# Seven instead of six pairs of hidden blocks by seven products, and the products of the edge rows in the next half's first steps

## The chip, the cores and the metric

The kernel runs on one core of one Trainium2 chip. The metric is the device time of one execution in microseconds (us), as the median of several runs. Five engines work beside each other, each with an instruction queue of its own: TensorE (PE in the profile, with its weight loads as PEld), VectorE (DVE), ScalarE (ACT), GpSimd (POOL) and SyncE (SP), which here issues nearly all transfers between memory and the core.

## What is computed

An attention with packed keys, followed by a gated feed-forward layer. For 8 batches of 8 heads, 576 rows of 64: 32 rows `p` attend to `k`, `v`; then `q` attends to the 32 packed rows. The result, 4608 rows of 512, goes through the feed-forward layer:

```python
p_packed = sm_attn(p, k, v)
out = sm_attn(q, p_packed, p_packed)
...
h = x @ w_in                      # 512 -> 2048
g = h * np.clip(h + 3.0, 0.0, 6.0) / 6.0
return (g @ w_out).astype(np.float32)   # 2048 -> 512
```

All in 32-bit floats. A number of full precision is kept as a high part, rounded to the format that TensorE reads, and a low part, the rest; a product of two such numbers takes three TensorE products (high by high, high by low, low by high).

## The kernel before

**Stages.** The first batch, with the loading and splitting of all weights, follows an order written out by hand (`PLAN`). After it comes a loop over the batches 1 to 7. Each has two *halves*, c = 0 and c = 1, of about 256 rows each, and each half goes through the 16 blocks of 128 hidden columns (d_ff = 2048) in 16 *steps* (`pos` in `moe_pairs`). The attention of the next batch is woven into the steps by `fill`, which calls generators: the loads and transposes of `attention_inputs` in steps 0 to 4 of the first half, then `attention`, and in the second half `u_s2` and the projections of the packed rows (`first_quarters`, with reloads of w_in, `w_again`). Outside the parts marked as manual, the framework orders the instructions of each engine itself when it builds the program, by dependencies and by the order in which they were written; on the chip each engine then follows that order strictly.

**A step.** `first_product` (L922) makes one block of h for the rows of the half: six TensorE products of 256 columns, or 320 in a *wide* half. `gate_into` (L938) applies the gate, on ScalarE and VectorE. Then the block is either a *single* or one of a *pair*:

- A single (`gated`, then `single_product`, L1162): the two blocks of 128 rows are split into high and low parts, and each is multiplied by the block's 512 columns of w_out: six products of 512 columns. They add into the banks A and B.
- A pair of blocks 2i and 2i + 1 (`pair_product`, L1130) is a 2 by 2 block product (two blocks of rows, two blocks of d_ff, two halves of the 512 output columns) by seven products in place of eight: sums of the gated blocks are made on VectorE (L1196, L1204, L1209) and split (`parted`, L949), and 21 products of 256 columns add into the banks A, B, C and D. After the last pair of a half, ScalarE, GpSimd and VectorE read C and D (L1148 to L1160); A and B are read after the last single (L1167).

A product is written out one or two steps after its block was gated (`pend`, `second`). The pairs come first in a half, then the singles: with six pairs, steps 0 to 11 and 12 to 15. The first half takes the pairs in descending order (5 to 0), the second in ascending order. The second half of batch 1 has four pairs, its first half none (`moe`, L1014).

**The combined blocks.** Of the weights of a pair, three sums (T1, T2, T4) have a place of their own, and a fourth (T3) takes the place of a block of w_out. `combine` (L1057) makes them during batch 1. There are four places for T1, T2 and T4, in the buffers that w_in held before, so that four of the pairs take turns in two of them: pairs 0 and 4 in one, 1 and 5 in the other. These four are kept in memory (`t_kept`, L1100), and `fetch_t` (L1103) brings them back, 768 KB each, by two fetches in each half (`FETCHES`, at steps 5 and 7), issued on SP.

**Edge rows.** A batch has 576 rows, 64 more than four blocks of 128. The 64 odd rows of an even batch and those of the odd batch behind it make one block of 128. Their gated columns are collected in `bnd` (`keep_edge`, L964), and in the first half of batches 3, 5 and 7 (`joined`) their products are made: eight *edge steps* of two d_ff blocks each, with parts split by `edge_parts` (L988) into a buffer that the pairs use too (`raw`), and multiplied by `edge_product` (L1000). They are written out between the singles of that half (L1225 to L1240), in the bank of D (in batch 7 in a bank of the attention), which ScalarE reads at the end (L1181).

Of the kernel before, what the change touches and what calls it, by code (L numbers as in the profile page):

```python
# [26 lines left out]
PAIRS = 6  # L27
FIRST_PAIRS = 4
TURN = (
# [3 lines left out]
FETCHES = (((5, 1), (7, 0)), ((5, 4), (7, 5)))  # L33
# [44 lines left out]
def packed_attention_moe(  # L78
# [420 lines left out]
    def u_a(b, x, z):  # L499
# [20 lines left out]
        hi = ap.tile([P, S], F32R, name="a_hi", tag=f"a_hi{x}", bufs=2)  # L520
        lo = ap.tile([P, S], F32R, name="a_lo", tag=f"a_lo{x}", bufs=2)
# [466 lines left out]
    def edge_parts(f, summed):  # L988

        j = xp.tile([P, 6 * P], F32R, name="edge", tag="raw")  # L990
        hi, lo = j[:, :3 * P], j[:, 3 * P:]
# [65 lines left out]
    def combine(i):  # L1057

        if i == 0:
            tiles = [wr.tile([P, 4, 2, H2], F32R, name=f"wt{n}", tag=f"w_in{n}") for n in (1, 2, 3)]  # L1060
            for k, name in enumerate(("T1", "T2", "T4")):
                for pair in range(PAIRS):
                    n, at = ((0, k), (1, k), (2, k), ((2, 0, 1)[k], 3))[pair % 4]
# [35 lines left out]
        if i % 4 < 2:  # L1099
            nc.sync.dma_start(out=t_kept[i % 4 + i // 4 * 2], in_=slots[i % 4].rearrange("p a x m -> p (a x m)"))  # L1100
        yield

    def fetch_t(i):  # L1103
        nc.sync.dma_start(out=slots[i % 4].rearrange("p a x m -> p (a x m)"), in_=t_kept[i % 4 + i // 4 * 2])

    def moe_pairs(b, c, fill):

        pairs = list(range(FIRST_PAIRS if b == 1 else PAIRS))
        if c == 0:
            pairs.reverse()  # L1110
        n_pairs = len(pairs)
        steps = [2 * i + k for i in pairs for k in range(2)] + list(range(2 * n_pairs, NF))
# [10 lines left out]
        edges = []  # L1123
# [6 lines left out]
        def pair_product(i, lhs):  # L1130
# [5 lines left out]
            if i == pairs[0]:  # L1136
                order = order[2:4] + order[:2] + order[4:]
# [34 lines left out]
        def edge_step(f, summed, parts):  # L1172
            if "J" not in made:
                made["J"] = att_pair()[0] if b == B - 1 else acc_of(roles[3])
                first = True
            else:
                first = False
            edge_product(made["J"], f, *parts, summed, first, f == NF - 2)
            if f == NF - 2:
                osb = gp.tile([P, DM], F32, name="osb_j", tag="g", bufs=4)  # L1180
                nc.scalar.activation(out=osb, in_=made["J"], func=AF.Copy, scale=1.0 / 6.0)  # L1181
                nc.sync.dma_start(out=out[b * S - REM:b * S + REM], in_=osb)

        for pos, f in enumerate(steps):
            fill(pos)
            h = first_product(b, f, t0, n)
            if pos < 2 * n_pairs:
                if f % 2 == 0:
# [9 lines left out]
                    second(1)  # L1198
                    continue
# [25 lines left out]
            if joined:  # L1225
                while edges:
                    edges.pop(0)()
            pend.append(lambda f=f, gh=gh, gl=gl: single_product(f, gh, gl))
            second(2)
            if joined:  # L1230
                j = f - 2 * n_pairs
                n_single = NF - 2 * n_pairs
                todo = [(2 * i, True) for i in range(n_pairs) if i * (n_single - 1) // n_pairs == j]
                if j == n_single - 1:
                    todo = [(g, False) for g in range(2 * n_pairs, NF, 2)]
                for g, summed in todo:
                    parts = edge_parts(g, summed)
                    edges.append(lambda g=g, summed=summed, parts=parts: edge_step(g, summed, parts))
        if joined:
            pend[-1:-1] = edges  # L1240
# [132 lines left out]
    t_kept = dram.tile([PAIRS - 2, P, 3 * DM], F32, name="t_kept")  # L1373
# [16 lines left out]
    for b in range(1, B):  # L1390
# [10 lines left out]
        def fill(c, f):  # L1401
            s = c * NF + f
            with behind_gates():
                if b == 1:
# [6 lines left out]
                    for i in range(PAIRS):  # L1411
# [58 lines left out]
```

## Time and profile before

| | before |
|---|---|
| runs | 715.52, 712.47, 714.78 us; median 714.78 us |
| profiled execution | 714.05 us; its span, first to last instruction, 712.2 us |
| mean granted clock of TensorE | 0.99 of full speed |
| instructions | 16078, of them 5906 TensorE products |
| transfers | 107.48 MB, 151 GB/s on average |

How to read the profile's lines: a group's line names the program's line, engine, operation, what is written and read, the shapes and the count; behind the bar stand its busy time in us, the mean of one in ns, and the idle time of the engine just before it with what ended it. A timeline's line has the start and the length in us, and behind the instruction in brackets the idle time before it. The chain is the sequence of work that ended last, followed back from the last instruction. A stretch's line has busy us and counts of PE, PEld, DVE, ACT and POOL, then the granted clock and the transfers. TensorE's products overlap, and their ends are modelled, so that their starts tell more than their lengths. `acc<-wt,gf` is a product of a pair that reads a combined block, `acc<-wo_hi,g` one of a single, `acc<-wo_hi,edge` one of an edge step.

### The profile page before, as it was taken

What the parts mean: (1) busy time and instruction counts of PE and PEld (TensorE: products, weight loads), DVE (VectorE), ACT (ScalarE), POOL (GpSimd) and SP (SyncE); (2) the same over time, 40 slices, a digit from 0 to 9 for tenths busy, and PEclk for the clock granted to TensorE, in tenths of its full rate; (3) what the DMA queues carried; (4) which work ended last, traced back from release to release, by engine and by line L of the source; (5) the groups of instructions that cost most, each with busy time, mean ns of one, the idle gap of its engine ahead of it and who ended that gap; (6) DMA issues with size and microseconds to landing.
All of it is one profiled execution on the core that took longest, in us unless ns stands there. A gap on an engine that the chain in (4) does not pass through costs nothing.

```text
span 712.2 us, 16078 instructions
## 1 busy us (share of the span) xinstructions
PE 691.6 (97%) x5906; PEld 594.8 (84%) x5906; DVE 532.0 (75%) x1169; ACT 428.6 (60%) x1013; POOL 353.6 (50%) x539
## 2 busy tenths in 40 slices
PE   6699999999999999999999999999999999999997
PEld 5477876888878888899798988899888898889997
DVE  3888788587899779786598867888488876975453
ACT  4798876556565655665366655657356564756453
POOL 1456642555353454465353534556354444547553
PEclk9799999999999999999999999999999999999999
DMA  9969953855327756474554657375543745331030
GB/s 264 338 153 273 217 149 119 258 152 117 108 106 196 169 137 209 118 175 76 129 193 136 161 116 222 109 154 139 130 164 119 165 122 178 119 134 46 30 105 29
DMA packets 199102, 107.48 MB, mean 151 GB/s; under 512 B 173424, under 2 KB 185200, under 8 KB 195440
## 3 DMA queue, kind: packets, MB, share of 16 engines
q1 hardware_dynamic: 198480, 106.26, 54.4%
q8 instruction: 46, 0.75, 0.5%
q14 instruction: 32, 0.26, 0.1%
q10 hardware_dynamic: 544, 0.20, 0.1%
HBM read 89.65 MB, written 16.78 MB: 149 GB/s over the span
## 4 chain that ended last, share of the span: by engine, by line
PE 87%; DVE 6%; DMA 4%; ACT 1%; issue 1%; SPq 1%; POOL 0%; DVEq 0%; ACTq 0%
PE acc L969 48%; PE ps_hh L929 23%; PE ps L350 5%; PE ps_h L607 4%; PE ps L969 2%; PE ps L470 1%; DMA nat<-in_k_dram 1%; DMA wt<-t_kept 1%; PE ps L440 1%; DVE tr L555 1%; PE ps_t L678 1%; DMA k_nat<-in_k_dram 1%; SPq L294 1%; PE ps L273 1%; DMA w_again<-w_kept 1%
## 5 line engine op out<-in xcount | busy, mean ns | idle before, releaser
L929 PE MATMUL ps_hh<-a_hi,m_hi 128*128 128x320 f32 (+1 forms) x448 | 134.8, 301 | 1.5 <-PE acc L969 0.8
L929 PE MATMUL ps_hh<-a_lo,m_hi 128*128 128x320 f32 (+1 forms) x448 | 133.9, 299 | 0.0
L929 PE MATMUL ps_hh<-a_hi,m_lo 128*128 128x320 f32 (+1 forms) x448 | 133.4, 298 | 0.0
L941 DVE SCALAR_TENSOR_TENSOR t<-t,ps_hh 128x320 f32<-128x320 f32 (+1 forms) x148 | 66.0, 446 | 58.9 <-ACT t L940 58.3
L947 POOL TENSOR_TENSOR gf<-tb,gf 128x256 fp32r<-128x256 f32 x76 | 64.6, 851 | 87.4 <-ACT gf L946 56.2
L969 PE MATMUL acc<-wo_hi,g 128*128 128x512 f32 x288 | 103.1, 401 | 0.0
L940 ACT ACTIVATE t<-ps_hh,three 128x320 f32<-128x320 f32 (+1 forms) x148 | 73.9, 500 | 35.0 <-PE ps_hh L929 29.0
L929 PEld LDWEIGHTS ps_hh<-a_hi,m_hi 128*128 128x128 f32 x448 | 85.2, 190 | 10.0 <-issue 3.0
L929 PEld LDWEIGHTS ps_hh<-a_lo,m_hi 128*128 128x128 f32 x448 | 85.2, 190 | 6.5 <-issue 3.5
L929 PEld LDWEIGHTS ps_hh<-a_hi,m_lo 128*128 128x128 f32 x448 | 85.1, 190 | 2.9 <-issue 2.5
L947 POOL TENSOR_TENSOR g<-t,g 128x256 fp32r<-128x256 f32 x72 | 55.7, 775 | 45.4 <-ACT g L946 23.3
L969 PE MATMUL acc<-wt,ga 128*128 128x256 f32 x456 | 74.6, 284 | 0.2
L969 PE MATMUL acc<-wo_hi,ge 128*128 128x256 f32 x304 | 71.5, 286 | 0.2
L947 POOL TENSOR_TENSOR ga<-t,ga 128x256 fp32r<-128x256 f32 x76 | 62.4, 821 | 13.6 <-ACT ga L946 12.3
L969 PEld LDWEIGHTS acc<-wt,ga 128*128 128x128 f32 x456 | 63.0, 190 | 3.3 <-ACT ga L946 1.7
L969 PEld LDWEIGHTS acc<-wo_hi,g 128*128 128x128 f32 x288 | 53.0, 189 | 13.7 <-POOL g L947 3.0
L969 PEld LDWEIGHTS acc<-wo_hi,ge 128*128 128x128 f32 x304 | 52.9, 189 | 8.6 <-ACT t L940 2.1
L965 POOL COPY bnd<-t 128x64 f32<-128x64 f32 x76 | 23.0, 302 | 70.2 <-DVE t L941 64.4
L969 PE MATMUL acc<-wo_lo,g 128*128 128x512 f32 x144 | 56.9, 395 | 0.0
L555 DVE STREAM_TRANSPOSE tr<-nat 128x576 f32<-128x576 f32 x56 | 42.3, 764 | 17.4 <-DMA nat<-in_q_dram 11.8
L940 ACT ACTIVATE tb<-ps_hh,three 128x256 f32<-128x256 f32 (+1 forms) x76 | 37.8, 498 | 19.5 <-PE ps_hh L929 18.5
L946 ACT CAST g<-t 128x256 fp32r<-128x256 f32 x72 | 29.2, 407 | 33.6 <-DVE t L941 33.0
(222 smaller groups left out, 1840.4 us busy)
## 6 DMA issues: line engine op xcount, KB each, us to landing
w_again<-w_kept SPq DMA_DIRECT2D x24, 1024.0 KB, 4.9
wt<-t_kept SPq DMA_DIRECT2D x24, 768.0 KB, 5.4
out_dram<-osb SPq DMA_DIRECT2D x33, 256.0 KB, 2.5
nat<-in_k_dram SPq DMA_DIRECT2D x112, 72.0 KB, 3.2
nat<-in_q_dram SPq DMA_DIRECT2D x112, 72.0 KB, 2.7
raw_in<-in_moe_w_in_dram SPq DMA_DIRECT2D x10, 512.0 KB, 5.2
raw_out<-in_moe_w_out_dram SPq DMA_DIRECT2D x10, 512.0 KB, 5.3
w_kept<-w_in_sb SPq DMA_DIRECT2D x4, 1024.0 KB, 9.4
```

Source lines behind the costliest of these rows:

```text
L273: nc.tensor.matmul(banks[x][NPK * a:NPK * a + NPK, :n * P], state["pp"][half, NPAIR * x + a], cols[half, :, a], start=True, stop=True,)
L294: nc.sync.dma_start(out=t[r:r + 32], in_=src[b, 2 * a + h, :, 32 * c:32 * c + 32].rearrange("(t i) j -> i t j", i=32),)
L350: nc.tensor.matmul(pair[x][NPK * a:NPK * a + NPK, :n], rows[half, a], c, start=True, stop=True)
L555: nc.vector.transpose(out=t, in_=state.pop(("nat", which, b, a)))
L607: nc.tensor.matmul(h[:, hf, :HS], mm[:, g, fs], aa[:, hf * HS:(hf + 1) * HS], start=(g == 0 and i == 0), stop=(g == NG - 1 and i == 2),)
L929: state["first"] = nc.tensor.matmul(h[:, :n], mm[:, g, fs], aa[:, t0:t0 + n], start=(g == 0 and i == 0), stop=(g == NG - 1 and i == 2),)
L940: state["relu"] = nc.scalar.activation(out=t[:, :n], in_=h, func=AF.Relu, bias=three)
L941: state["gate"] = nc.vector.scalar_tensor_tensor(out=t[:, :n], in0=t[:, :n], scalar=6.0, in1=h, op0=ALU.min, op1=ALU.mult)
L946: nc.scalar.copy(out=hi, in_=x)
L947: engine.tensor_sub(out=lo, in0=x, in1=hi.bitcast(F32))
L965: nc.gpsimd.tensor_copy(out=bnd[:, f, side * REM:side * REM + REM], in_=t[:, boff:boff + REM])
L969: nc.tensor.matmul(out, lhs[x], rhs[y], start=first and i == 0, stop=last and i == 2, skip_group_check=True)
```

## The change

- `PAIRS` goes from 6 to 7: the halves of batches 2 to 7 have seven pairs and two singles, but for the first half of batch 2, which keeps six and four, since pair 6 is combined in its steps 12 to 15 (`TURN_LAST`). The order is 5 to 0, then 6 in the first half; 6, then 0 to 5 in the second.
- `PLACE` says which of the four places a pair's blocks have: pairs 0 and 4 share one, 2, 5 and 6 another, and 1 and 3 keep theirs. Five pairs are kept in memory (`KEPT`). There are three fetches in a half: at step 5 pair 2 in both halves, at step 7 pair 0 or 4, at step 11 pair 6 or 5.
- The products of the edge rows are no longer written out in the first half of batches 3, 5 and 7. `owe`, at the end of that half, makes a list of the eight edge steps, and `owed` issues one, two and three of them in the first three steps of the next half and the rest in the fourth. Their parts lie in the buffers of the next batch's attention weights (`a_hi`, `a_lo`), which are empty until then.
- The first pair of a half makes its product for D fourth instead of second.

```diff
-PAIRS = 6
+PAIRS = 7
 FIRST_PAIRS = 4
+PLACE = (1, 3, 0, 2, 1, 0, 0)
+KEPT = (0, 2, 4, 5, 6)
...
+TURN_LAST = (12, 12, 12, 13, 13, 14, 15)
...
-FETCHES = (((5, 1), (7, 0)), ((5, 4), (7, 5)))
+FETCHES = (((5, 2), (7, 0), (11, 6)), ((5, 2), (7, 4), (11, 5)))
+EDGES = (1, 2, 3)
...
-        hi = ap.tile([P, S], F32R, name="a_hi", tag=f"a_hi{x}", bufs=2)
-        lo = ap.tile([P, S], F32R, name="a_lo", tag=f"a_lo{x}", bufs=2)
+        hi, lo = state.pop(("a_room", b, x), None) or (
+            ap.tile([P, S], F32R, name=f"a_{z}", tag=f"a_{z}{x}", bufs=2) for z in ("hi", "lo")
+        )
...
-        if i % 4 < 2:
-            nc.sync.dma_start(out=t_kept[i % 4 + i // 4 * 2], in_=slots[i % 4].rearrange("p a x m -> p (a x m)"))
+        if i in KEPT:
+            nc.sync.dma_start(out=t_kept[KEPT.index(i)], in_=slots[PLACE[i]].rearrange("p a x m -> p (a x m)"))
...
+    def owe(b, pairs):
+
+        rooms = []
+        for x in range(2):
+            t = [ap.tile([P, S], F32R, name=f"a_{z}", tag=f"a_{z}{x}", bufs=2) for z in ("hi", "lo")]
+            rooms.append([z[:, :3 * P] for z in t])
+            if b < B - 1:
+                state["a_room", b + 1, x] = t
+        todo = [(2 * i, True) for i in pairs] + [(f, False) for f in range(0, NF, 2) if f // 2 not in pairs]
...
+        for i, (f, summed) in enumerate(todo):
+            def prepared(i=i, f=f, summed=summed):
+                parts = edge_parts(f, summed, rooms[i % 2])
+                return lambda: edge(f, summed, parts, i)
+            edges.append(prepared)
+        for _ in range(2):
+            ready.append(edges.pop(0)())
+
+    def owed(count):
+
+        while ready and count:
+            count -= 1
+            ready.pop(0)()
+            if edges:
+                ready.append(edges.pop(0)())
...
-        pairs = list(range(FIRST_PAIRS if b == 1 else PAIRS))
-        if c == 0:
-            pairs.reverse()
+        last = PAIRS - 1
+        if b == 1:
+            pairs = list(range(FIRST_PAIRS))
+        elif c == 0:
+            pairs = list(range(last - 1, -1, -1)) + [last] * (b > 2)
+        else:
+            pairs = [last] + list(range(last))
...
-                order = order[2:4] + order[:2] + order[4:]
+                order = order[2:3] + order[:2] + order[3:]
...
                 pend.append(lambda i=f // 2, lhs=lhs: pair_product(i, lhs))
+                if pos >= len(EDGES):
+                    owed(NF)
                 second(1)
+                if pos < len(EDGES):
+                    owed(EDGES[pos])
                 continue
...
+            if joined and pos == NF - 1:
+                owe(b, pairs)
...
                     for at, i in FETCHES[c]:
-                        if f == at:
+                        if f == at and (b, c, i) != (2, 0, PAIRS - 1):
                             fetch_t(i)
+                    if b == 2:
+                        for _ in range(TURN_LAST.count(s)):
+                            next(turned[PAIRS - 1], None)
```

More of the change, by code (lines that the diff above doesn't have):

```diff
@@ L986, in acc_of, with edge_parts @@
         return ps_o.tile([P, DM], F32, name="acc", tag=f"acc{i}", bufs=1)
-    def edge_parts(f, summed):
-        j = xp.tile([P, 6 * P], F32R, name="edge", tag="raw")
-        hi, lo = j[:, :3 * P], j[:, 3 * P:]
+    def edge_parts(f, summed, rooms=None):
+        if rooms:
+            hi, lo = rooms
+        else:
+            j = xp.tile([P, 6 * P], F32R, name="edge", tag="raw")
+            hi, lo = j[:, :3 * P], j[:, 3 * P:]
         raw = bnd[:, f:f + 2]
@@ L1062, in combine @@
                 for pair in range(PAIRS):
-                    n, at = ((0, k), (1, k), (2, k), ((2, 0, 1)[k], 3))[pair % 4]
+                    n, at = ((0, k), (1, k), (2, k), ((2, 0, 1)[k], 3))[PLACE[pair]]
                     blocks[pair, name] = [tiles[n][:, at, x] for x in range(2)]
@@ new lines, in packed_attention_moe, with edge @@
+    edges, ready = [], []
+    def owe(b, pairs):
[6 more added lines that the diff above has]
+        todo = [(2 * i, True) for i in pairs] + [(f, False) for f in range(0, NF, 2) if f // 2 not in pairs]
+        made = []
+        def edge(f, summed, parts, i):
+            if not made:
+                made.append(att_pair()[0] if b == B - 1 else acc_of(roles[3]))
+            acc, = made
+            done = i == len(todo) - 1
+            edge_product(acc, f, *parts, summed, i == 0, done)
+            if done:
+                osb = gp.tile([P, DM], F32, name="osb_j", tag="g", bufs=4)
+                nc.scalar.activation(out=osb, in_=acc, func=AF.Copy, scale=1.0 / 6.0)
+                nc.sync.dma_start(out=out[b * S - REM:b * S + REM], in_=osb)
+        for i, (f, summed) in enumerate(todo):
[5 more added lines that the diff above has]
+            ready.append(edges.pop(0)())
@@ L1111, in moe_pairs @@
+    def owed(count):
[4 more added lines that the diff above has]
+                ready.append(edges.pop(0)())
+    def moe_pairs(b, c, fill):
+        last = PAIRS - 1
[3 more added lines that the diff above has]
+            pairs = list(range(last - 1, -1, -1)) + [last] * (b > 2)
+        else:
+            pairs = [last] + list(range(last))
         n_pairs = len(pairs)
-        steps = [2 * i + k for i in pairs for k in range(2)] + list(range(2 * n_pairs, NF))
+        steps = [2 * i + k for i in pairs for k in range(2)]
+        steps += [f for f in range(NF) if f not in steps]
@@ L1170, in single_product @@
                     nc.sync.dma_start(out=out[row + k * P:row + (k + 1) * P], in_=r)
[L1172 to L1182, printed above, removed]
         for pos, f in enumerate(steps):
@@ L1198, in moe_pairs @@
                     second(1)
+                    owed(EDGES[pos] if pos < len(EDGES) else 0)
                     continue
@@ L1372, in packed_attention_moe @@
     w_kept = dram.tile([NCH, P, FPC * DM], F32, name="w_kept")
-    t_kept = dram.tile([PAIRS - 2, P, 3 * DM], F32, name="t_kept")
+    t_kept = dram.tile([len(KEPT), P, 3 * DM], F32, name="t_kept")
     def keep_w_in(n):
@@ L1410, in fill @@
                                 keep_w_in(n)
-                    for i in range(PAIRS):
+                    for i in range(PAIRS - 1):
                         for _ in range(TURN[i].count(s)):
```

19 lines of the change are left out of this document (2 added, 17 removed).

## The prediction, made before the change was run

> **What bounds the kernel now.** I read the page first: the busy shares and the chain that ended last.
>
> ```profile
> span 712.2 us, 16078 instructions
> PE 691.6 (97%) x5906; PEld 594.8 (84%) x5906; DVE 532.0 (75%) x1169; ACT 428.6 (60%) x1013; POOL 353.6 (50%) x539
> ...
> PE 87%; DVE 6%; DMA 4%; ACT 1%; issue 1%; SPq 1%; POOL 0%; DVEq 0%; ACTq 0%
> ```
>
> TensorE is busy 97% of the span and holds 87% of the chain. Its instructions overlap in this trace, so the busy share alone proves little. What shows the bound is the chain in order of time (start, length, what): in the steady part one group of products begins where the one before ends. I take from it the price of the two things that the change exchanges, and two more rows for later.
>
> ```profile
> 232.77 6.04 DMA wt<-t_kept
> ...
> 243.56 2.52 PE acc L969 x21
> ...
> 247.23 1.39 PE acc L969 x6
> ...
> 274.91 2.49 PE acc L969 x21
> ...
> 380.62 1.38 PE acc L969 x6
> ...
> 404.00 1.44 PE ps_hh L929 x12
> ```
>
> Six products of 512 columns (one block's second product in a half) take 1.38 or 1.39 us. The 21 products of 256 columns that replace two such blocks take 2.49 or 2.52 us. Starts follow columns: 1.385 / 6 = 0.231 us for 512, 2.505 / 21 = 0.119 us for 256. So the kernel is a queue of TensorE products, and a change pays by the products that it takes out of the queue, less the waits that it puts in.
>
> **The change part by part.**
>
> *The seventh pair.* Batches 2 to 7 have twelve halves. All but the first half of batch 2 (still six) get a seventh pair: 11 times two blocks' singles go, 2 x 1.385 = 2.77 us, and one pair comes, 2.505 us. That saves 0.265 us each, 2.9 us in all. By the extreme rows it is 11 x (2.76 - 2.52) = 2.6 to 11 x (2.78 - 2.49) = 3.2 us. The first products of both blocks stay as they are.
>
> The page "TensorE: Matmul & The Clock Gate" of the Trainium skill, section "Back-to-back issue gap", speaks against this: it gives a sustained spacing of 81 ns at 128 columns and 131 ns at 512. An estimate from that page, on a line between its two figures, is 98 ns at 256 columns: 21 x 98 = 2.05 us against 12 x 131 = 1.57 us, a loss of 0.48 us per pair and 5.3 us in all. The trace disagrees with it: 231 ns at 512 columns, 119 at 256.
>
> *VectorE, ScalarE, GpSimd for the seventh pair.* The groups by line and shape (busy us, mean ns) of narrow halves:
>
> ```profile
> L1209 DVE TENSOR_TENSOR tb<-tb,t 128x128 f32<-128x128 f32 x76 | 44.6, 587 | 1.4
> ...
> L947 DVE TENSOR_TENSOR ge<-t,ge 128x256 fp32r<-128x256 f32 x76 | 36.8, 484 | 10.8 <-ACT ge L946 9.2
> ...
> L1204 DVE TENSOR_TENSOR t<-t,tb 128x256 f32<-128x256 f32 x76 | 35.4, 466 | 0.8
> ...
> L941 DVE SCALAR_TENSOR_TENSOR t<-t,ps_hh 128x256 f32<-128x256 f32 x72 | 29.6, 412 | 21.9 <-ACT t L940 21.6
> ...
> L1196 DVE TENSOR_TENSOR t<-t 128x128 f32<-128x128 f32 x76 | 24.1, 317 | 2.0
> ...
> L1076 DVE TENSOR_TENSOR wt<-wx,wt 128x256 fp32r<-128x256 f32 x18 | 7.9, 439 | 3.2 <-ACT wt L1075 2.9
> ```
>
> Two singles cost VectorE two gates, 0.82 us. A pair costs two gates and four more instructions: 0.82 + 0.587 + 0.484 + 0.466 + 0.317 = 2.68 us. So 1.86 us are added per half, where the busiest half is a second one (c = 1) with the next batch's attention. The stretches of 5 us there (PE, PEld, DVE, ACT, POOL busy):
>
> ```profile
> 447.00:452.00 5.00, 5.00 (x48) 4.16 (x48) 5.00 (x12) 2.71 (x9) 3.68 (x6) 1.00 0.54 192
> 452.00:457.00 5.00, 5.00 (x36) 4.76 (x35) 4.18 (x8) 4.18 (x10) 2.97 (x6) 1.00 0.06 23
> 457.00:462.00 5.00, 5.00 (x37) 3.33 (x36) 3.01 (x8) 2.82 (x6) 2.21 (x6) 1.00 0.31 92
> ```
>
> VectorE is full to 452 us, while TensorE still loses nothing. The seventh pair falls into the next two rows, which leave 0.82 + 1.99 = 2.81 us idle. That covers 1.86 us, so I cost it at nothing; if the cover is gone, it is 1.86 us in each of six second halves, 11.2 us. ScalarE gets four casts for two, GpSimd three subtractions for two; at 60% and 50% of the span I cost both at nothing.
>
> *Pair 6 is combined once,* in steps 12 to 15 of batch 2's first half: 11 more VectorE instructions of about 0.44 us (the L1076 row), 4.8 us, beside the four singles that stay in that half. Nothing, at most 4.8 us if none of it were hidden.
>
> *Edge rows.* Three times (batches 3, 5, 7) one of eight edge steps turns from six products of 512 columns into three of 512 and six of 256: 3 x 0.231 + 6 x 0.119 - 1.385 = 0.02 us each, 0.1 us together. Where the steps run hardly changes. The TensorE timeline of batch 3, and ScalarE's read of the sum:
>
> ```profile
> 331.58 0.28 PE L929 MATMUL ps_hh<-a_hi,m_hi 128*128 128x256 f32 x1
> ...
> 332.30 0.40 PE L969 MATMUL acc<-wo_hi,edge 128*128 128x512 f32 x1
> ```
> ```profile
> 353.71 0.60 ACT L1181 ACTIVATE osb_j<-acc 128x512 f32<-128x512 f32 x1 [1.59 <-PE acc L969]
> ```
>
> The 256-column first product of 331.58 us belongs to the next half. So the edge products run in the next half's first steps today: the order that the framework builds had already put them there. The new place of their parts frees a buffer of the pairs, for which TensorE did not wait in these rows. The sum's bank must be read before the first pair's fourth product uses it; the new order puts nine products of 0.119 us in front, 1.07 us for a read of 0.60 us. Nothing; at most 0.6 us three times.
>
> *The fetches.* They grow from 24 to 35, and one more store. What hurts is when each is needed. In a first half the fetch at step 5 now brings pair 2, used as the fourth pair, where before it brought pair 1, the fifth. It stands on SP behind the attention loads of five steps. SP's timeline, batches 4 and 6, then TensorE's first product that reads a fetched place, in the fourth pair of its half in batches 2, 4 and 6 (234.97, 402.16, 569.34), and in the fifth of batch 2 (238.86); then the page's transfers:
>
> ```profile
> 397.19 1.27 SPq L409 DMA_DIRECT2D v_nat<-in_v_dram  x2
> 398.56 1.83 SPq L1104 DMA_DIRECT2D wt<-t_kept  x2
> ...
> 566.39 1.02 SPq L1104 DMA_DIRECT2D wt<-t_kept  x2
> ```
> ```profile
> 234.97 0.52 PE L969 MATMUL acc<-wt,gf 128*128 128x256 f32 x3
> ...
> 238.86 0.62 PE L969 MATMUL acc<-wt,gf 128*128 128x256 f32 x3 [0.26 <-DMA wt<-t_kept]
> ...
> 402.16 0.52 PE L969 MATMUL acc<-wt,gf 128*128 128x256 f32 x3
> ...
> 569.34 0.52 PE L969 MATMUL acc<-wt,gf 128*128 128x256 f32 x3
> ```
> ```profile
> w_again<-w_kept SPq DMA_DIRECT2D x24, 1024.0 KB, 4.9
> wt<-t_kept SPq DMA_DIRECT2D x24, 768.0 KB, 5.4
> ```
>
> Issued as now, the fetch of batch 2 lands at 232.77 + 6.04 = 238.81, 3.84 us after the fourth pair wants it at 234.97. In batch 4 it lands at 398.56 + 5.4 = 403.96 for 402.16, 1.80 us late; in batch 6 at 571.79 for 569.34, 2.45 us late. Batches 3 and 5 I take at the mean of the last two, 2.1 each (an estimate); batch 7 has no attention to load. Together 12.3 us late, if nothing else changes. Against it: 12 of a pair's 21 products read no fetched place (12 x 0.119 = 1.43 us), and the next two steps' 12 first products, 1.44 us by the row at 404.00, can stand in front. The framework orders the queue when it builds it, and did so freely (edge products, above). If it knows of the late landing, 2.87 us of cover hides all but 3.84 - 2.87 = 0.97 us in batch 2. If it doesn't, the queue waits, as in the row of 238.86. From 0 to 12.3 us I take 1.0 us, since the rows around it show a queue without gaps, and keep both ends.
>
> The new fetch at step 11 (pair 5 in second halves, 6 in first) must land before step 15. In first halves SP is idle by then. In second halves it may stand behind a w_again load. The time that it has is two pairs, by TensorE's timeline of batch 4:
>
> ```profile
> 446.62 0.40 PE L969 MATMUL acc<-wt,gf 128*128 128x256 f32 x2
> ...
> 451.63 0.40 PE L969 MATMUL acc<-wt,gf 128*128 128x256 f32 x2
> ```
>
> One pair is 5.01 us, two are 10.0; the two transfers, end to end, are 4.9 + 5.4 = 10.3 us. Nothing, at most 0.3 us in six halves, 1.8 us.
>
> *The end.* Two singles instead of four now follow the last pair. Its last product, the last of the three reads of banks C and D, and the last reads of A and B:
>
> ```profile
> 701.29 0.28 PE L969 MATMUL acc<-wo_hi,ga 128*128 128x256 f32 x1
> ```
> ```profile
> 703.69 0.42 DVE L1153 SCALAR_TENSOR_TENSOR osb<-acc,osb 128x256 f32<-128x256 f32 x1
> ```
> ```profile
> 707.89 1.38 DVE osb L1167 x2
> ```
>
> The reads of C and D ended at 704.11, 2.7 us after the last pair's last product had gone in (701.29 + 0.12), long before those of A and B could start at 707.89. With two singles behind the pair, A's last product has gone in 2.77 - 0.69 = 2.08 us after it, so the reads of C and D end up to 0.6 us late. Part of their 2.7 us is a gate that VectorE will have done earlier. I take 0.2 us, from 0 to 0.6.
>
> **The sum:** -2.9 + 0.1 + 0.2 + 1.0 = -1.6 us. The profiled execution took 714.05 us (span 712.2 and 1.85 around it), so 712.45 on its own terms. It lay 0.73 us below the median shown, 714.78; for the median I say 713.2.
>
> **Rivals.**
>
> *The fourth pair waits for its fetch* (slower). For: the three late sums above, and a queue that stands still at 238.86 with products behind it that need no fetch. Against: the order may be rebuilt around it. The gain before this wait is 2.6 us; beyond that it is slower than before. Half of the 12.3 us uncovered gives 714.78 - 2.6 + 6.2 = 718.4, all of it 724.5.
>
> *VectorE becomes the bound of second halves.* For: 5.00 of 5 us to 452. Against: the two rows after it. Half a microsecond in six halves eats the gain: 715.2; all 11.2 us would be 723.4.
>
> *All is hidden.* 2.9 or 3.2 us less: 711.6 to 711.9.
>
> *Weight loads, one per product, set the spacing:* then 21 loads for 12 lose. For: loads are busy 84% of the span. Against: six products take 1.385 us, not the 0.71 of six at 0.119. Were it so, nine more loads of 0.119 us in 11 pairs cost 11.8 us: 726.6. The page of the Trainium skill cited above is the case for it.
>
> *The change doesn't do what it says* only in its second part: the edge products stay about where they are.
>
> **How the numbers follow.** About 0.5% (3.6 us) is what a measurement of this kernel can tell from no change: below 711.2 is faster, above 718.4 slower. The forecast with small waits, 711.9 to 715, has 0.58; all hidden 0.14; VectorE 0.10; the fetch wait 0.16; loads 0.02. Faster: even the full gain reaches 711.6 only, so it needs the spread of runs (712.47 to 715.52 before) on its side: 0.20. Slower: the fetch wait, mostly, and the loads: 0.17. Same: 0.63. The range starts a microsecond under the full gain, 710.6, and goes past the half-uncovered fetch, 719.0; outside it lies the fully uncovered one.
>
> **What would show it.** Right: 2 x 11 x 6 = 132 fewer 512-column products on `g`, 231 more of 256; 35 fetches; the first fourth-pair fetch product with at most a microsecond of wait. Wrong: a releaser "DMA wt" of many microseconds on TensorE or its loads in first halves (the fetch), gaps ending on VectorE or ScalarE around steps 10 to 15 of second halves, a 21-product row far from 2.5 us, or a tail over half a microsecond longer.

## The result, and the profile after

| | before | after |
|---|---|---|
| median of 6 runs | 713.54 us (712.11 to 715.52) | 721.32 us (720.37 to 725.59) |
| profiled execution, its span | 714.05, 712.2 us | 721.55, 719.8 us |
| ratio | | 1.0121, 95% interval 1.0088 to 1.0153 |

The change makes the kernel 7.8 us slower, outside the range given (710.6 to 719.0). (One execution of e9 below and the traced one of e14 ran far longer than the others of their kernels; the ratios leave them out, and no trace of e14 is read.) Two lines of the page's head, the chain's shares, and the group of products that read the fetched places:

```profile
span 719.8 us, 16493 instructions
...
PE 691.9 (96%) x6014; PEld 599.8 (83%) x6014; DVE 552.8 (77%) x1227; ACT 436.8 (61%) x1042; POOL 364.5 (51%) x555
...
PE 72%; DVE 12%; DMA 8%; ACT 3%; issue 2%; SPq 2%; POOL 1%; DVEq 0%; ACTq 0%; POOLq 0%
...
L977 PE MATMUL acc<-wt,gf 128*128 128x256 f32 x261 | 54.5, 286 | 6.7 <-DMA wt<-t_kept 6.7
```

TensorE's share of the chain falls from 87% to 72%, VectorE's and the transfers' rise to 12% and 8%. The products themselves are what was forecast. First the products of singles and one group of those of pairs before, then after (a line's products by tile: count, ns, first and last start):

```profile
L969 PE MATMUL acc<-wt,ga x456: 274/283/387, 178.7 to 700.9; 128*128 128x256 f32 x152
...
L969 PE MATMUL acc<-wo_hi,g x288: 387/394/502, 123.9 to 708.2; 128*128 128x512 f32 x144
...
L969 PE MATMUL acc<-wo_lo,g x144: 387/394/496, 124.1 to 707.9; 128*128 128x512 f32 x144
```
```profile
L977 PE MATMUL acc<-wt,ga x522: 276/283/415, 178.8 to 711.8; 128*128 128x256 f32 x174
...
L977 PE MATMUL acc<-wo_hi,g x200: 387/394/502, 124.0 to 714.8; 128*128 128x512 f32 x100
...
L977 PE MATMUL acc<-wo_lo,g x100: 388/394/496, 124.2 to 714.6; 128*128 128x512 f32 x100
```

(288 + 144) - (200 + 100) = 132 products of 512 columns are gone; `acc<-wt,ga` has 66 more, six for each of 11 pairs, so 231 of 256 columns have come. Against them stand these five starts on TensorE's timeline, one in the first half of each of batches 2 to 6, and the sum of the weight loads' waits for the same thing (us, times, longest):

```profile
238.14 0.39 PE L977 MATMUL acc<-wt,gf 128*128 128x256 f32 x1 [1.35 <-DMA wt<-t_kept]
...
317.03 0.39 PE L977 MATMUL acc<-wt,gf 128*128 128x256 f32 x1 [0.61 <-DMA wt<-t_kept]
...
406.33 0.39 PE L977 MATMUL acc<-wt,gf 128*128 128x256 f32 x1 [1.35 <-DMA wt<-t_kept]
...
486.38 0.39 PE L977 MATMUL acc<-wt,gf 128*128 128x256 f32 x1 [1.51 <-DMA wt<-t_kept]
...
576.51 0.39 PE L977 MATMUL acc<-wt,gf 128*128 128x256 f32 x1 [1.89 <-DMA wt<-t_kept]
```
```profile
PEld acc L977 <- DMA wt<-t_kept: 7.8, 5, 2.1
```

In starts of products the five waits are 7.5 us (1.51 + 0.77 + 1.51 + 1.67 + 2.05: the distance to the product before, less the usual one of its kind); before there was one of 0.4 us. All five stand at the fourth pair, for pair 2. Why the fetch is late is seen on SP's timeline of batch 4 (start, length, how many issues):

```profile
387.09 1.96 SPq L301 DMA_DIRECT2D nat<-in_k_dram  x4
389.14 0.92 SPq L1225 DMA_DIRECT2D out_dram<-osb  x2
390.15 1.00 SPq L426 DMA_DIRECT2D v_nat<-in_v_dram  x2
391.24 2.32 SPq L301 DMA_DIRECT2D nat<-in_k_dram  x4
393.66 2.07 SPq L301 DMA_DIRECT2D nat<-in_q_dram  x4
395.77 1.79 SPq L426 DMA_DIRECT2D v_nat<-in_v_dram  x2
397.67 2.06 SPq L301 DMA_DIRECT2D nat<-in_q_dram  x4
399.78 1.27 SPq L416 DMA_DIRECT2D v_nat<-in_v_dram  x2
401.14 6.88 SPq L1115 DMA_DIRECT2D wt<-t_kept  x3
```

SP does not pause: 24 issues in the 14.05 us from 387.09 to 401.14, 0.59 us each, and the fetch is the 25th. It lands 5.1 us later, at 406.28, and the waiting product starts at 406.33.

What covers a late fetch can be counted on TensorE. In every one of the five halves the fourth pair has issued its three products on `wo` and `gf` when it wants the fetched place. In batch 4 the third of them, and the last product ahead of the waiting one, are

```profile
403.62 0.29 PE L977 MATMUL acc<-wo_hi,gf 128*128 128x256 f32 x1
...
404.69 0.28 PE L937 MATMUL ps_hh<-a_hi,m_lo 128*128 128x256 f32 x1
```

so the place is wanted at 403.62 + 0.12 = 403.74, and the fetch is 2.54 us late. In batches 2 to 6 the five fetches are 3.50, 1.24, 2.54, 1.86 and 3.09 us late, 12.2 us together. Between the third product and the waiting one stand 17, 4, 9, 2 and 9 others: 41 x 0.119 = 4.9 us of cover. The difference, 7.3 us, is what TensorE waits (7.5 in starts).

The end is longer too. The reads of A, then C or D, then B:

```profile
714.55 0.69 DVE L1222 SCALAR_TENSOR_TENSOR osb<-acc,osb 128x512 f32<-128x512 f32 x1 [0.23 <-PE acc L977]
...
714.81 0.40 PE L977 MATMUL acc<-wo_hi,g 128*128 128x512 f32 x1
715.16 0.41 DVE L1208 SCALAR_TENSOR_TENSOR osb<-acc,osb 128x256 f32<-128x256 f32 x1
...
715.68 0.69 DVE L1222 SCALAR_TENSOR_TENSOR osb<-acc,osb 128x512 f32<-128x512 f32 x1
```

The third read of C and D (L1208) now falls between those of A and B (L1222). From TensorE's last start to the end of the span it is 719.76 - 714.81 = 4.95 us; before it was 712.23 - 708.15 = 4.08. Half of the difference is this order: the last read ends 1.56 us after TensorE's last start (714.81 to 716.37), before it was 1.12. The other 0.4 us lie behind the last read; no run explains them.

So the account is -2.9 (products) + 7.1 (more waits for fetches) + 0.9 (end) = +5.1 us of the 7.8. Some 3 us more were still to be found.

### The profile page after: what moved, and what is told of

Same layout as the page of the kernel before. It is cut to its first block, busy times and chain, and to the rows that moved or that the text cites. A ratio compares the mean times of both kernels' runs of the same rounds, so it can differ in the third digit from the quotient of the medians.

```text
span 719.8 us, 16493 instructions
## 1 busy us (share of the span) xinstructions
PE 691.9 (96%) x6014; PEld 599.8 (83%) x6014; DVE 552.8 (77%) x1227; ACT 436.8 (61%) x1042; POOL 364.5 (51%) x555
## 4 chain that ended last, share of the span: by engine, by line
PE 72%; DVE 12%; DMA 8%; ACT 3%; issue 2%; SPq 2%; POOL 1%; DVEq 0%; ACTq 0%; POOLq 0%
PE acc L977 39%; PE ps_hh L937 19%; PE ps L357 4%; DMA wt<-t_kept 4%; PE ps_h L615 3%; DMA nat<-in_k_dram 2%; PE ps L977 2%; SPq L301 1%; PE ps L477 1%; DVE t L949 1%; DMA w_again<-w_kept 1%; DVE wt L1087 1%; DVE tr L563 1%; DMA raw_in<-in_moe_w_in_dram 1%; PE ps_t L686 1%
## 5 line engine op out<-in xcount | busy, mean ns | idle before, releaser
L955 POOL TENSOR_TENSOR gf<-tb,gf 128x256 fp32r<-128x256 f32 x87 | 74.2, 853 | 124.2 <-ACT gf L954 85.9
L977 PE MATMUL acc<-wt,ga 128*128 128x256 f32 x522 | 87.2, 287 | 0.2 <-ACT ga L954 0.2
L977 PE MATMUL acc<-wo_hi,ge 128*128 128x256 f32 x348 | 82.6, 285 | 0.9 <-ACT ge L954 0.8
L977 PEld LDWEIGHTS acc<-wt,ga 128*128 128x128 f32 x522 | 72.7, 191 | 7.2 <-POOL bnd L973 2.5
L977 PE MATMUL acc<-wo_hi,g 128*128 128x512 f32 x200 | 71.2, 398 | 0.0
L977 PEld LDWEIGHTS acc<-wo_hi,ge 128*128 128x128 f32 x348 | 61.0, 190 | 9.3 <-ACT gf L954 4.2
L977 PE MATMUL acc<-wt,gf 128*128 128x256 f32 x261 | 54.5, 286 | 6.7 <-DMA wt<-t_kept 6.7
L954 ACT CAST ge<-t 128x256 fp32r<-128x256 f32 x87 | 35.3, 405 | 25.0 <-DVE t L1239 23.4
L955 DVE TENSOR_TENSOR ge<-t,ge 128x256 fp32r<-128x256 f32 x87 | 42.3, 486 | 10.5 <-ACT ge L954 9.8
L954 ACT CAST gf<-tb 128x256 fp32r<-128x256 f32 x87 | 35.3, 405 | 24.0 <-DVE tb L949 22.4
```

What stands on the lines that cost most here:

```text
L954: nc.scalar.copy(out=hi, in_=x)
L955: engine.tensor_sub(out=lo, in0=x, in1=hi.bitcast(F32))
L977: nc.tensor.matmul(out, lhs[x], rhs[y], start=first and i == 0, stop=last and i == 2, skip_group_check=True)
```

## The experiments

All differ from the changed kernel, or from the one before where that is said, by the lines shown. Times are medians; the ratio is to the kernel before on the same chip.

| | us | ratio (95% interval) |
|---|---|---|
| e1_fetch_step4 | 713.60 | 1.0011 (0.9992 to 1.0029) |
| e2_pair2_fifth | 717.44 | 1.0066 (1.0042 to 1.0090) |
| e3_edges_only | 712.86 | 0.9993 (0.9976 to 1.0009) |
| e4_six_fourth | 719.33 | 1.0085 (1.0054 to 1.0115) |
| e5_early_cd | 713.35 | 1.0013 (0.9997 to 1.0030) |
| e6_three_places | 714.14 | 1.0025 (1.0010 to 1.0039) |
| e7_three_cd | 713.09 | 1.0011 (0.9996 to 1.0026) |
| e8_fetch_act | 723.65 | 1.0187 (1.0154 to 1.0220) |
| e9_seven_no_fetch | 712.98 | 1.0007 (0.9988 to 1.0026) |
| e10_six_no_fetch | 712.89 | 0.9991 (0.9973 to 1.0010) |
| e11_early_cd_pool | 712.23 | 0.9992 (0.9976 to 1.0007) |
| e12_t_last | 723.10 | 1.0146 (1.0106 to 1.0187) |
| e13_six_more_vector | 720.86 | 1.0107 (1.0091 to 1.0123) |
| e14_seven_no_fetch_pool | 709.30 | 0.9934 (0.9917 to 0.9952) |
| e15_three_cd_pool | 713.69 | 1.0008 (0.9993 to 1.0023) |
| e16_early_cd_pool_all | 710.53 | 0.9955 (0.9941 to 0.9969) |
| e17_six_pool | 713.49 | 1.0000 (0.9986 to 1.0015) |
| e18_cd_pool_late | 719.76 | 1.0107 (1.0073 to 1.0140) |

### Is it the late fetch?

**Issue it a step earlier.**

```diff
-FETCHES = (((5, 2), (7, 0), (11, 6)), ((5, 2), (7, 4), (11, 5)))
+FETCHES = (((4, 2), (7, 0), (11, 6)), ((5, 2), (7, 4), (11, 5)))
```

> The changed kernel with the fetch of pair 2 in first halves at step 4 instead of 5, so that it is issued ahead of two of the attention loads; nothing else. Fetch theory: the five waits on the fetch in batches 2 to 6 (7.5 us together) fall to under 2 us and the time falls by 5 to 7 us, to about 715. Rival (the seventh pair's vector work, the moved edge steps and the end make the loss, and TensorE would only wait for something else at the same place): the waits on the fetch go, others of like size take their place, and the time stays above 719.

713.6 us: 7.7 less than the changed kernel, and no wait on a fetch is left in its trace. But it is not faster than before (713.31 beside it): the 2.9 us do not show.

**Let pair 2 come fifth.**

```diff
-            pairs = list(range(last - 1, -1, -1)) + [last] * (b > 2)
+            pairs = [5, 4, 3, 1, 2, 0] + [last] * (b > 2)
...
-FETCHES = (((5, 2), (7, 0), (11, 6)), ((5, 2), (7, 4), (11, 5)))
+FETCHES = (((5, 2), (7, 0), (12, 6)), ((5, 2), (7, 4), (11, 5)))
```

> The changed kernel with first halves taking their pairs in the order 5, 4, 3, 1, 2, 0, 6, so that the pair that is fetched at step 5 comes fifth, as before the change, and the pair that has a place of its own comes fourth; the fetch of pair 6 moves from step 11 to 12, behind the use of its place. Fetch theory: the same as with the earlier issue, 5 to 7 us less, about 715, with under 1 us of waits on the fetch, though the fetch is issued as late as in the changed kernel. Rival: above 719. If pair 6's later fetch comes too late, a new wait on a fetch stands at the last pair of first halves.

717.44: half a hit. The waits on fetches fall to 0.3 us, but TensorE waits for something new (its waits: us, times, longest):

```profile
PE ps L477 <- DMA v_high<-in_v_dram: 1.9, 5, 0.6
```

In starts of products of this form 3.6 us are lost. The fetch moved to step 12 is now issued ahead of the loads of q and v of the next stage.

**One thing of the change in the kernel before.**

```diff
+PLACE = (1, 3, 0, 2, 1, 0)
+KEPT = (0, 2, 4, 5)
-FETCHES = (((5, 1), (7, 0)), ((5, 4), (7, 5)))
+FETCHES = (((5, 2), (7, 0)), ((5, 4), (9, 5)))
...
```

> The kernel before with one thing of the change: its four places are dealt out so that in first halves the pair fetched at step 5 is pair 2, the fourth, and not pair 1, the fifth. Six pairs, edge steps as before, two fetches in each half (in second halves the one of pair 5 at step 9, since its place is free later). Fetch theory: waits on the fetch of 6 to 8 us in batches 2 to 6 and a time of 719 to 722, slower than before without a seventh pair. Rival: about 714, and the waits only appear along with the seventh pair.

719.33, six pairs all the same. Its waits:

```profile
PE acc L971 <- DMA wt<-t_kept: 6.4, 5, 3.3
```

So the late fetch alone costs 6 us and needs no seventh pair.

**The edge steps alone:** six pairs with places, fetches and order of before (`PAIRS = 6`, `PLACE = (0, 1, 2, 3, 0, 1)`), and `owe`, `owed` and the product for D fourth as in the change.

> Only the second part of the change: six pairs with the fetches, places and order of before, the edge steps issued in the next half's first steps and the first pair's product for D fourth. If the moved edge steps cost nothing, as predicted: 712.5 to 714.5. If they are part of the loss (one stall in each of three halves and the parts made later), 715 or more.

712.86, as before. The moved edge steps are out of it.

### Queue or transfers, and what covers the fetch

**The fetch on another queue.**

```diff
...
-                            fetch_t(i)
+                            fetch_t(i, nc.scalar if (c, at) == (0, 5) else nc.sync)
```

> The changed kernel with the fetch at step 5 of first halves issued on ScalarE's queue instead of SP's; where it is written stays the same. If it is SP's queue that makes the fetch late (some twenty issues of about half a microsecond stand ahead of it): the fetch starts some microseconds earlier, the waits of 7.5 us fall to under 3, and the time to 715 to 717. If it is the transfers themselves (the memory side full with the loads): it starts earlier and lands no earlier, and the time stays at 719 to 722.

723.65, worse than the change. The fetch of batch 2 on ScalarE's queue, then VectorE:

```profile
225.78 0.36 ACTq L1115 DMA_DIRECT2D wt<-t_kept  x1
...
232.48 0.78 DVE L563 STREAM_TRANSPOSE tr<-nat 128x576 f32<-128x576 f32 x1 [3.74 <-DMA nat<-in_k_dram]
```

It is issued 6.6 us earlier than in the changed kernel (232.37 there), and TensorE waits for no fetch. But its 768 KB now move beside the small loads of k: the last of these, issued at 225.71, lands at 232.35, 6.6 us later (in the changed kernel 226.00 and 229.77, 3.8 us). The transpose that stands at the head of VectorE's queue idles 3.74 us for it, the gates behind it are late, and TensorE waits 2.8 us for one there. In all, its waits for gates are 10.1 us in starts, for 1.5 in the changed kernel: 8.6 us more, where the fetch had cost 7.5. Neither of the two expectations names this. The Trainium skill, page "DMA: Bandwidth & Descriptors", section "Issuing engines are not separate DMA queues", says that transfers of all issuing engines run on the same 16 DMA engines and interleave, and that another issuer saves only the time of issuing. This trace agrees: the issue is 6.6 us earlier, and the loads pay. The section also calls the issue time usually small beside the transfer. So it is here for one transfer, 0.59 us for 5.1; it is 24 issues in a row that take 14 us.

The early fetch of e1 has a like chain on a smaller scale, VectorE first, then TensorE:

```profile
395.10 0.78 DVE L563 STREAM_TRANSPOSE tr<-nat 128x576 f32<-128x576 f32 x1 [1.28 <-DMA nat<-in_k_dram]
395.80 0.38 DVE L949 SCALAR_TENSOR_TENSOR tb<-tb,ps_hh 128x256 f32<-128x256 f32 x1
```
```profile
396.24 0.39 PE L937 MATMUL ps_hh<-a_hi,m_hi 128*128 128x256 f32 x1 [0.45 <-DVE tb L949]
```

But most of this is not the fetch: in e9 below, without any fetch, the same transpose waits 1.06 us (at 393.67) and TensorE 0.23 behind it.

**Products that need no fetch first.**

```diff
+            if i != pairs[0]:
+                order = [order[k] for k in (0, 2, 3, 6, 1, 4, 5)]
```

> The changed kernel with the products of all pairs but the first of a half in another order: the four that read no fetched place first, the three that read T4, T1 and T2 last. The fetches stay at step 5. In the changed kernel only the three products of A12 and B21 stand ahead of T4; now twelve do, nine more of 0.119 us, 1.07 us of cover in each pair. If TensorE follows the written order inside a pair, each of the five waits of 0.77 to 2.05 us falls by 1.07 us, to 2.6 us in all, and the time by 4.9 us, to 716 to 717. If the order in which the queue is built already covers what it can, no change: 720 to 722.

723.1: no gain, but the new order did not arrive on TensorE where it was meant to. Batch 4 on TensorE and on SP:

```profile
407.00 0.52 PE L977 MATMUL acc<-wt,gf 128*128 128x256 f32 x2 [1.72 <-DMA wt<-t_kept]
```
```profile
401.89 1.02 SPq L1115 DMA_DIRECT2D wt<-t_kept  x2
```

Ahead of the waiting product stand the same products as in the changed kernel: three of the pair on `gf`, three on `ga` and six first products of a later step. It is so in batches 2 and 6 too; in batch 3 one fewer stands there, in batch 5 one more. The order that the framework builds had kept its place for the fetched products, so whether more cover would help was not tested. In batch 4 the fetch came 0.75 us later and the wait is as long as before; the five waits are 5.9 us in starts instead of 7.5, and the time does not follow.

### Where do the saved products go?

**Three places taking turns,** so that the four pairs in place come first in every half (e6); then with C and D first in a half's last pair (e7, the second piece of code). e5 has this order with the early fetch of e1.

```diff
-PLACE = (1, 3, 0, 2, 1, 0, 0)
-KEPT = (0, 2, 4, 5, 6)
+PLACE = (1, 3, 0, 2, 1, 0, 2)
+KEPT = (0, 2, 3, 4, 5, 6)
...
-FETCHES = (((5, 2), (7, 0), (11, 6)), ((5, 2), (7, 4), (11, 5)))
+FETCHES = (((5, 2), (7, 0), (9, 6)), ((5, 3), (7, 4), (9, 5)))
...
-            pairs = list(range(last - 1, -1, -1)) + [last] * (b > 2)
+            pairs = [5, 4, 3, 1, 2, 0] + [last] * (b > 2)
...
-            pairs = [last] + list(range(last))
+            pairs = [6, 0, 2, 1, 3, 4, 5]
```
```diff
+            if i == pairs[-1]:
+                order = order[2:6] + order[:2] + order[6:]
```

> The changed kernel with three instead of two of the four places taking turns, first halves in the order 5, 4, 3, 1, 2, 0, 6 and second halves 6, 0, 2, 1, 3, 4, 5, with fetches at steps 5, 7 and 9: in every half the four pairs that are in place come first, each fetch is needed two or more pairs after it is issued, and in first halves the fetch at step 5 stays behind the attention loads on SP. Theory (SP's queue has room for the fetch only behind those loads; ahead of them it delays the gates through VectorE, at step 12 it delays the loads of v): waits on fetches under 0.5 us, waits on a transpose at the head of VectorE as before the change, no wait on v; so the 2.9 us of the seven products show: 711.5 to 712.5 with the longer end, 1 to 2 under before. Rival (VectorE is full with the seventh pair and TensorE waits for gates wherever the fetch is): 713 to 715 with 2 us or more of waits on gates.

> The one with three places taking turns, and in the last pair of every half the products for C and D ahead of those for A and B. Theory: 0.7 to 1.0 us under the one with three places, 710.5 to 711.7, faster than both kernels. Rival: no better than three places alone.

> The changed kernel with the fetch of pair 2 at step 4, and in the last pair of every half the four products for C and D ahead of the three for A and B. Theory (the longer end comes from the reads of C and D, which start 9 products too late now that two singles follow the last pair): A's last read is no longer followed by a wait for the third read of C and D, the time from the last product's start to the end falls from 5.0 to about 4.2 us, and the time is 0.7 to 1.0 us under the one with the early fetch alone, about 712.8. Rival (the end is set by the last product and the store): the end stays at 5.0 us, no change.

All three miss their times: 714.14, 713.09 and 713.35, none faster than before. The part on the end can be seen in the traces only: from TensorE's last start to the end 4.4 us in e5 (4.96 without the order), 4.3 in e7 (4.7 in e6); the runs do not separate half a microsecond. In e15, e16 and e18 below, which have this order too, it is 4.6 to 4.7.

**No fetch at all,** with seven pairs and with six (`pass` in place of `fetch_t(i)`).

> The changed kernel without any of its 35 fetches, so that four of the seven pairs are multiplied by weights of other pairs; all else as in the changed kernel. The longest wait that fetches can cause, on TensorE or through delayed loads on VectorE, is gone. Theory (what is left of the loss with the early fetch comes from the transfers): about 2 us under the kernel before without its fetches (2.9 us of products saved, 0.9 us of a longer end). Rival (it comes from VectorE's extra work in the seventh pair): within 1 us of it, with waits of TensorE on gates of 2 us or more.

> The kernel before without any of its 24 fetches, so that two of the six pairs are multiplied by weights of other pairs; the counterpart of the changed kernel without fetches. Both theories: the kernel before waited 0.4 us for fetches, so 0 to 1.5 us less than before, 711.5 to 713; its distance to the other is what tells.

712.98 and 712.89: without a single fetch, seven pairs are still no faster than six. So the transfers are not what keeps the gain. TensorE's waits for gates, with seven, then with six:

```profile
PE ps_hh L937 <- DVE tb L949: 1.5, 5, 0.4
```
```profile
PE ps_hh L929 <- DVE tb L941: 0.4, 1, 0.4
```

In starts, all waits that end on a gate of VectorE are 1.1 us in the kernel before, 1.1 with six pairs here and 2.6 with seven. Five of the six with seven pairs stand in first halves, 13 to 16 us after the batch's first product.

**More work on VectorE alone,** in the kernel before: five instructions on unused columns, at steps 12 and 13.

```diff
+            if b > 1 and f in (12, 13):
+                a1, a2, a = (t[:, off + i * P:off + j * P] for i, j in ((0, 1), (1, 2), (0, 2)))
+                if f == 12:
+                    nc.vector.tensor_sub(out=t[:, W:W + P], in0=a2, in1=a1)
+                nc.vector.tensor_add(out=t[:, W:W + 2 * P], in0=a, in1=a)
+                nc.vector.tensor_sub(out=t[:, W:W + 2 * P], in0=a, in1=a)
```

> The kernel before with five more VectorE instructions in the first two singles (steps 12 and 13) of each half from batch 2 on, about 2.2 us in each half by the rows of such instructions (0.317 and 4 x 0.466), on columns that nothing reads. VectorE theory: the gates behind them come late in the batches with attention; 1.5 to 4 us more than before, 714 to 717. Rival (VectorE has room for it, as predicted): within 0.7 us of before.

720.86: 7.5 us slower, nearly twice the highest expected. The groups of the added instructions, and a stretch of VectorE and TensorE in batch 5:

```profile
L1232 DVE TENSOR_TENSOR t<-t 128x256 f32<-128x256 f32 x24 | 16.0, 678 | 0.0
L1233 DVE TENSOR_TENSOR t<-t 128x256 f32<-128x256 f32 x24 | 14.5, 615 | 0.1
L1231 DVE TENSOR_TENSOR t<-t 128x128 f32<-128x128 f32 x12 | 3.4, 283 | 0.0
```
```profile
472.95 0.78 DVE L555 STREAM_TRANSPOSE tr<-nat 128x576 f32<-128x576 f32 x1 [2.23 <-DMA nat<-in_k_dram]
473.65 0.65 DVE L539 TENSOR_TENSOR m_lo<-ps,m_hi 128x512 fp32r<-128x512 f32 x1
474.22 0.40 DVE L947 TENSOR_TENSOR ge<-t,ge 128x256 fp32r<-128x256 f32 x1
```
```profile
474.68 0.38 PE L969 MATMUL acc<-wo_hi,ge 128*128 128x256 f32 x1 [1.46 <-DVE ge L947]
```

33.9 us of VectorE work in 12 halves, 2.8 each, cost 7.5 us in a kernel whose VectorE is busy 75% of the span. In this stretch the delay comes in the next half: VectorE has idled 2.23 us for a load of k and is still at a transpose and a split of the attention when the pair's split is wanted. In starts, waits that end on a gate or a split of VectorE are 5.7 us in all (1.1 before). The added instructions also hold the buffer of the gates; that was not separated from their time.

**Less work on VectorE:** the low part of `ge` on GpSimd, in first halves only (e11) or in all (e14, e16 to e18, e15).

```diff
-                    parted(lhs, ("A11", "S3"), gp.tile([P, 4 * P], F32R, name="ge", tag="g", bufs=4), columns[:, :, :P], nc.vector)
+                    parted(lhs, ("A11", "S3"), gp.tile([P, 4 * P], F32R, name="ge", tag="g", bufs=4), columns[:, :, :P])
```

(In e11 the last argument is `nc.vector if c else nc.gpsimd`.) e11 and e16 are e5 with this move, e14 is e9 with it, e17 the kernel before with it.

> The changed kernel with the fetch of pair 2 at step 4 and C and D first in the last pair, and besides with the first split of each pair in first halves (the low part of ge) on GpSimd instead of VectorE: seven times 0.4 to 0.5 us less on VectorE in each first half, 0.8 us more on GpSimd each. Rival (VectorE full): waits of TensorE on gates fall from some 2.6 us to under 1, and the time by 1 to 2 us to about 711.5. Transfer theory (gates wait behind a transpose that waits for its load): the waits on gates stay, and GpSimd's longer path adds some; 713 to 715.

> Seven pairs without fetches (four pairs are multiplied by weights of other pairs) and with the low part of ge made on GpSimd in all halves. VectorE theory: some 3 us less VectorE work in each half than without this move, so the saved products show: 2 to 3 us under the same without the move (712.98), 710 to 711. Rival: no change, 712 to 714.

> The changed kernel with the fetch of pair 2 at step 4, C and D first in the last pair, and the low part of ge on GpSimd in all halves. VectorE theory: 1 to 2 us under the one that moves it in first halves alone (712.23), 710 to 711.5, and faster than the kernel before by 0.2 to 0.4%. Rival: 712 to 713.5.

> The kernel before, six pairs, with the low part of ge on GpSimd in all halves; nothing of the change. VectorE theory: TensorE hardly waited for gates before (1.4 us in all), so it gains at most 1 us: 712 to 713. Rival (the move helps by itself, whatever the number of pairs): 710 to 711.5.

VectorE's theory holds in all four, though e14 gains more than the 2 to 3 us expected and e17 lies 0.5 us over its range. Without fetches the time falls from 712.98 to 709.30. With the early fetch it falls from 713.35 to 712.23 (first halves) and 710.53 (all): faster than both kernels, by 0.45% of the one before. With six pairs the same move gives nothing (1.0000; its trace holds one wait of 1.2 us on a fetch, so up to 0.2% may be hidden there). The page of e16, and GpSimd's group:

```profile
span 708.3 us, 16530 instructions
...
PE 689.1 (97%) x6014; PEld 598.4 (84%) x6014; DVE 524.0 (74%) x1140; ACT 437.8 (62%) x1042; POOL 427.0 (60%) x642
...
PE 84%; DMA 5%; DVE 4%; ACT 2%; POOL 2%; issue 1%; SPq 0%; ACTq 0%; POOLq 0%; DVEq 0%
```
```profile
L955 POOL TENSOR_TENSOR ge<-t,ge 128x256 fp32r<-128x256 f32 x87 | 68.4, 786 | 81.1 <-ACT ge L954 35.1 <-issue 24.1 <-PE acc L977 7.9
```

VectorE's share of the chain falls from 12% to 4%, and in this trace no wait of TensorE from batch 2 on ends on a gate of VectorE (2.6 us in e9). The Trainium skill, page "GPSIMD Engine Reference", section "4.1 Engine selection", puts elementwise work on VectorE, since GpSimd is about half as fast. The trace has 786 ns for 484 (L947 before), 1.6 times; yet the slower engine is the right one here, since it has the room.

**Both causes, and the two cures together.** e18 keeps the fetch at step 5, e15 takes three places; both have C and D first and `ge` on GpSimd.

> The changed kernel with its fetches as they are (pair 2 at step 5 of first halves), C and D first in the last pair, and the low part of ge on GpSimd in all halves. If the late fetch and VectorE's load are two causes that add up: 7 to 8 us over the one with the early fetch (710.53), 717 to 719, with 6 us or more of waits on fetches. If the gates that come late and the fetches that come late hide each other: 712 to 716.

> Three places taking turns (fetches at steps 5, 7 and 9, the four pairs in place first), C and D first in the last pair, and the low part of ge on GpSimd in all halves. If a fetch ahead of the attention loads still costs something once VectorE is relieved: under the one with the early fetch, 709 to 710.5. If not: within 0.7 us of it, 710 to 711.3.

e18 gives 719.76, 9.2 over e16; its waits on fetches:

```profile
PE acc L977 <- DMA wt<-t_kept: 7.0, 5, 2.3
```

The two causes do not hide each other: e18 lies above the 717 to 719 that their sum gave, by less than its four runs differ (716.6 to 722.5). e15 misses: 713.69, 3.2 over e16. In its trace batches 2 to 7 are 2.2 us longer than in e16's (494.2 for 492.0): pair 2, now fifth, still waits 2.1 us for the fetch at step 5. The rest stands ahead of batch 2.

The batches tell the same story without the noise of the start, one trace each. Length from a batch's first product to the next one's, for batch 7 to TensorE's last start, in us:

```
batch                       2      3      4      5      6      7    2 to 7
before                  79.71  89.05  77.85  89.00  77.95  81.52   495.08
after                   81.78  89.19  79.29  90.32  81.34  81.05   502.97
e10 six, no fetch       80.06  88.88  78.25  88.93  77.64  81.52   495.28
e9 seven, no fetch      80.53  88.75  77.88  88.87  78.06  81.07   495.16
e13 six, more VectorE   81.13  90.53  78.93  91.74  79.67  81.51   503.51
e16 early, GpSimd       79.29  88.26  77.45  88.23  77.67  81.08   491.98
```

Batch 7 has no attention beside it. There the seven pairs of after, e9 and e16 save 0.44 to 0.47 us, and more VectorE work costs nothing. In batches 2 to 6 the saving of these rows shows only in e16. Such sums carry an error of 1 us or more: the six-pair kernels before, e3, e10 and e17 have 494.7 to 495.7, e6 has 493.1 and e7, which differs by one order, 496.4.

## Why the prediction was wrong

- **The bound and the products: right.** 132 and 231 products, and 0.45 us in batch 7 for two pairs at 0.265. In e16, batches 2 to 7 are 3.1 us shorter than before, for the 2.9 forecast and 0.4 of a wait that is gone. The rival of weight loads (726.6) is refuted: e14 and e16 are faster with the 108 more loads.
- **The fetch wait, +1.0 of 0 to 12.3: the step that failed.** The late sum was right, 12.2 us in the trace of after for 12.3. The cover was not: "2.87 us of cover hides all but 3.84 - 2.87 = 0.97 us in batch 2" counts 24 products in every batch, and the framework put 41 in front in all five, 4.9 us or 1.0 us a batch. So 7.5 us were left instead of 1.0. Three of the 24, those on `wo` and `gf`, stood in front in the rows of before already (234.51 to 234.85 in batch 2); for the rest the sum chose the case in which the framework puts all of them there. The first rival had the mechanism and its price, 718.4 to 724.5, with a chance of only 0.16.
- **VectorE at nothing: the second step that failed.** The reading "which leave 0.82 + 1.99 = 2.81 us idle. That covers 1.86 us" takes idle time in a window for room. The size of the work was about right: VectorE's busy time rose by 20.8 us, for 11 x 1.86 = 20.5 and 4.8 for combining pair 6. But the gate of a step is wanted at a given moment. The window shown was one of a second half, and the gates came late in first halves, beside the attention (five of e9's six waits). Seven against six pairs without fetches: 0.1 us shorter over batches 2 to 7 instead of 2.9, so about 2.8 us were given back; e13, e14 and e16 show that it is VectorE's load. 1.5 us of it are seen as waits for gates (2.6 for 1.1); the traces do not name the rest. The second rival named this (715.2 for half a microsecond in six halves), though it looked for it in second halves only.
- **The edges, +0.1, and the order of their products: right,** as far as a time can tell (e3).
- **The end, +0.2 of 0 to 0.6: too small.** 0.9 us. The reads of C and D were not only late by the 0.6 us that the sum allowed: the third of them fell between A's and B's and held the latter up, for 0.4 us; the other 0.4 us are not explained.
- **The fetch at step 11 and the combining of pair 6: right,** no wait for either in the trace of after.

The sum with what was measured is -2.9 + 7.1 + 0.9 + 2.8 = 7.9, for 7.8 us. That it fits to 0.1 us is luck: the 2.8 come from two single traces. In the traces of before and after, batches 2 to 7 are 7.9 us longer, the end 0.9, and what lies ahead of batch 2 is 1.2 us shorter.

What stays open: why work of 2.8 us in a half costs 0.75 us there (7.5 over the ten halves with attention). That VectorE frees the buffers of the next loads late, so that these are issued late and its next transposes wait, would fit the row of 472.95 us; it was not tried alone. Nor was it tried whether more products in front of the fetched ones would cover the fetch (e12 did not move them). Nor is it settled why three places are no better.

## What to carry to other kernels

A transfer that is wanted one step earlier has to be followed through its whole queue: count the issues ahead of it and their price, and ask what it displaces if it goes first. Cover counted from products that could stand in front holds only if they do: look at the order that was built. Idle time of an engine in a window is not room for more work; put the work there alone, without the gain, and time it. When a saving on the bounding engine does not show, look at a stretch where the others have little to do (here batch 7): if it shows there, the saving is real and something else spends it.

## What the runs showed of the hardware

Two prices were not expected. An issue costs SP 0.59 us, so that the 24 small transfers ahead of a fetch take longer to issue (14 us) than the fetch to land (5.1 us). And work of 2.8 us on an engine that is idle a quarter of the time can cost the kernel 0.75 us in each half, and nothing in halves without attention.
